# Retention and a Mish layer in one kernel: k cast to fp16 by GpSimd's transfers instead of by ScalarE, from the ninth chunk on

## The chip, the cores and the metric

The kernel runs on one core of a Trainium2 chip. The metric is the device time of one execution in microseconds. Before the change it is 204.29 us, the median of three runs (203.35, 204.29 and 204.36). The engines go by their names in the profile: PE is TensorE's matmul (PEld its weight load), DVE is VectorE, ACT is ScalarE, POOL is GpSimd and SP is SyncE, which here only issues transfers.

## The reference: what is computed

Four batches of eight heads go through a recurrent retention over 768 tokens, with head size 64. The result, as 3072 rows of 512, goes through a two-layer network with the activation h * tanh(softplus(h)) (Mish) between the layers.

```python
gamma = 1.0 - 2.0 ** (-5.0 - np.arange(H))
scale = 1.0 / np.sqrt(D)
for t in range(S):
    state = gamma[None, :, None, None] * state + np.einsum('bhd,bhe->bhde', k[:, :, t], v[:, :, t])
    y[:, :, t] = scale * np.einsum('bhd,bhde->bhe', q[:, :, t], state)
...
h = x @ w_in                                   # 512 x 2048
sp = np.where(h > 20.0, h, np.log1p(np.exp(np.minimum(h, 20.0))))
out = (h * np.tanh(sp)) @ w_out                # 2048 x 512
```

## The kernel before

**Chunks and blocks.** The recurrence is computed in 24 chunks of 128 tokens, six to a batch. Inside a chunk the scores k q^T are masked and multiplied by v ("present"); what came before the chunk enters as the state times q ("past"); the outer products of k and v and a decay give the next state. The decay inside a chunk is put into q and v as a factor per token and head (`qs` and `vs`, tables that the host makes), so k only needs the constant factor `BOOST` = 16, which keeps fp16 in its range. The network divides by BOOST cubed inside the Mish (`inv_boost3`). The network works on blocks of tokens: block 0 has four chunks, and the ten blocks after it have two each (`BLOCKS`, `first`). From block 1 on its first product, and from block 2 on its second too, are done with seven products of half size in place of eight (`g1_seven`, `seven`), which need sums of operands: `x_sums`, `sums_a`, `sums_b`, `sums_c` on VectorE.

**The way of q, k and v.** For chunk g, `load` asks SP for three transfers of 256 KB, each of 128 x 8 rows of 256 bytes. `cast_q` and `cast_v` multiply by the tables and give fp16 on GpSimd; `cast_k` scales by BOOST and gives fp16 on ScalarE (L334). q and k lie side by side in one tile (`qk16`, five buffers), which `turn_by_dma` transposes with one transfer on SP (L351) into `qkt`, where head size lies on partitions. Chunks 0 to 3 have a path of their own (`load_two`, `cast_two`, `turn_two`); chunks 4 and 5 are turned by TensorE.

**The order.** The program's order is written out by hand and each engine works its instructions off in that order. `g1_seven` and `seven` call `step(name)` at named places, and `steps_of(blk)` says which work of the retention stands there, with `a` = the block's first chunk + 4 and `nb` the next block. The places that matter here, in the order of a block:

- *p2*, early in the first product: GpSimd gets `gate_x`, the cast of q of chunk a, the decay of the next block's first state (`decay_next`, L417), the cast of v of chunk a. TensorE gets the outer products of the next block.
- *p6*: SP gets the transpose of chunk a and the loads of chunk a+3 (`turn_and_load`).
- *p7*, *p4*, *end*: stores, the second state's sum, and the sums for the second product on VectorE.
- *h2*: the scores of the next block.
- *m1*, in the second product: ScalarE gets the cast of k of chunk a+1.
- *m2*: GpSimd gets `gate_g`, the decay of the second state, and the casts of q and v of chunk a+1; SP the transpose of chunk a+1.
- *m7*: the next block's y, and ScalarE's cast of k of chunk a+2.
- *m3*: `x_sums` of the next block on VectorE.

A gate (`gate_x`, `gate_g`, L347) is a GpSimd copy of one element of the last result of a group of VectorE's sums. It holds GpSimd's queue until VectorE has done with them.

Block 1 has a half plan of its own: `steps_of_half` in the first product and `plan_of` in the second, which is plain.

Of the kernel before, what the change touches and what calls it, by code (L numbers as in the profile page):

```python
# [16 lines left out]
def kernel(  # L17
# [9 lines left out]
    nc = tc.nc  # L27
# [3 lines left out]
    C = 128  # L31
    NCH = S // C
    NCK = B * NCH
    HP = H // 2
    TB = 512
    CPB = TB // C
# [8 lines left out]
    BOOST = 16.0  # L45
    scale = float(1.0 / np.sqrt(D))
    inv_boost3 = float(1.0 / BOOST**3)

    gamma = (1.0 - 2.0 ** (-5.0 - np.arange(H))).astype(np.float64)
    jj = np.arange(C)  # L50
    mid = (C - 1) / 2.0
    qs_np = np.stack([BOOST * scale * g ** (jj - mid) for g in gamma], 1).astype(np.float32)
    vs_np = np.stack([BOOST * g ** (mid - jj) for g in gamma], 1).astype(np.float32)
    spread = [qs_np[(jj * CPB + r) % C] for r in range(CPB)]
    in_two = [vs_np[(jj % HB) * R + r] for r in range(R)]
# [57 lines left out]
    raw, k16s, v16s, t16s, kts, amf = {}, {}, {}, {}, {}, {}  # L113
    loaded, cast, qkts, ats, ams, states, us, ys, sus = {}, {}, {}, {}, {}, {}, {}, {}, {}
# [3 lines left out]
    nsnap = [0]  # L118
    SEVEN, HALF_SEVEN = 2, 1
    nload, late = [0], []  # L120
    stores = []

    def room(g):
        loaded[g] = [
            lpool.tile([P, H, D], FP32, name=nm + "f", tag=nm + "f", bufs=4 if nm == "q" else 6)
            for nm in "qkv"]

    def load_one(g, n, queue):  # L130
        b, c = divmod(g, NCH)
        queue.dma_start(
            loaded[g][n], (q, k, v)[n][b, :, c * C:(c + 1) * C].rearrange("h p d -> p h d"))

    def load(g):
        room(g)
        for n in (0, 1, 2) if g < CPB + 4 else (1, 0, 2):
            load_one(g, n, nc.sync)

    def load_to(g):  # L140
        while nload[0] < min(g, NCK):
            load(nload[0])
            nload[0] += 1
# [86 lines left out]
    def cast_two(nm, s, half):  # L230
        src = raw.pop((nm, s, half))
        if nm == "k":
            if s not in k16s:
                k16s[s] = castp.tile([P, 2, R, HP, D], FP16, name="qk16")
            nc.scalar.mul(k16s[s][:, half].rearrange("p r h d -> p h r d"), src, BOOST)  # L235
        else:
            v16s[s, half] = castp.tile([P, R, HP, D], FP16, name="v16")
            nc.gpsimd.tensor_tensor(
                v16s[s, half].rearrange("p r h d -> p h r d"), src,
                vs_two[:, half * HP:(half + 1) * HP].unsqueeze(3).broadcast_to((P, HP, R, D)),  # L240
                op=ALU.mult)
# [79 lines left out]
    def room16(g):  # L321
        if g not in cast:
            qk16 = castp.tile([P, 2, H, D], FP16, name="qk16")
            cast[g] = (qk16[:, 0], qk16[:, 1], castp.tile([P, H, D], FP16, name="v16"), qk16)
        return cast[g]

    def cast_q(g):
        if g < NCK:
            nc.gpsimd.tensor_tensor(  # L329
                room16(g)[0], loaded[g][0], qs.unsqueeze(2).broadcast_to((P, H, D)), op=ALU.mult)  # L330

    def cast_k(g):
        if g < NCK:
            nc.scalar.mul(room16(g)[1], loaded[g][1], BOOST)  # L334

    def cast_v(g):
        if g < NCK:
# [3 lines left out]
    def casts(g):  # L341
        cast_q(g)
        cast_k(g)
        cast_v(g)
# [160 lines left out]
    def mish(blk, u, h_ps):  # L505
        nt = BLOCKS[blk] * C
        per = TB // nt
        room = NFB * TB // (2 * nt)
        at0, lies = divmod(u * per, room)
        if lies == 0:  # L510
            gtiles[blk, at0] = gp.tile([P, room, nt], FP16, name="g", tag="g0" if blk == 0 else "g")
        gt = gtiles[blk, at0][:, lies:lies + per]
        nc.scalar.activation(gt, h_ps, AF.Mish, scale=inv_boost3)
        for j in range(per):
            gts[blk, u * per + j] = gt[:, j]
# [288 lines left out]
    def first_block():  # L804
# [15 lines left out]
        first_q_out(0, tq, nc.scalar)  # L820
        tq = [tq, turn_first_q(qf, 1)]
        cast_two("k", 0, 0)
        turn_two(0, 0)
        first_q_out(1, tq[1], nc.vector)
        turned_two(0, 0)
        cast_two("k", 0, 1)
        spin_wide(at, 3)
        scores_half(0, 0, at)
# [3 lines left out]
        for half in range(2):  # L832
            cast_two("v", 0, half)
# [112 lines left out]
    def steps_of(blk):  # L946
        a, nb = first[blk] + 4, blk + 1
        if nb == len(BLOCKS):
            only, then = lambda *work: [], lambda *work: []
        else:  # L950
            only = lambda *work: list(work)
            then = only if a < NCK else lambda *work: []
        return {
            "p2": [*then((gate_x, blk), (cast_q, a)), *only((outer_next, nb), (sum_next, nb, 0),
                   (decay_next, nb, 0)), (cast_v, a)],
            "p6": [(store_due, 1), (turn_and_load, a)],
            "p7": [(store_due, 2), *only((sum_next, nb, 1)), (sums_a, blk, slice(0, FPS))],
            "p4": [(store_due, 3), (sums_a, blk, slice(FPS, FPS + 2))],
            "h2": only((scores, a - 2), (scores, a - 1), (mask, a - 2)),
            "end": [(sums_a, blk, slice(FPS + 2, 2 * FPS))],  # L960
            "m1": [(cast_k, a + 1)],
            "m2": [*only((gate_g, blk), (decay_next, nb, 1)), (cast_q, a + 1), (cast_v, a + 1),
                   *only((mask, a - 1)), (turn_and_load, a + 1)],
            "m7": [*only((y_two, nb)), (cast_k, a + 2)],
            "m3": only((x_sums, nb)),
        }

    def steps_of_half(blk):
        a = first[blk] + 4
        return {  # L970
            "p2": [(gate_x, blk), (cast_v, a - 1)],
            "u2": [(cast_k, a - 1)],
            "p6": [(turn_and_load, a - 1), (some_late, 1)],
            "p7": [(cast_q, a), (some_late, 1)],
            "p4": [(cast_v, a), (some_late, 1), (store, 2)],
            "end": [(cast_k, a), (turn_and_load, a), (store, 2)],
        }

    def plan_of(blk):
        a = first[blk] + 4  # L980
        return {10: [(scores_two, blk + 1)],
                11: [(cast_q, a + 1), (cast_k, a + 1)],
                12: [(outer_two, blk + 1), (cast_v, a + 1), (turn_and_load, a + 1)],
                14: [(y_two, blk + 1)],
                15: [(cast_k, a + 2)]}

    first_block()
    x_sums(HALF_SEVEN)
# [1 line left out]
    for blk in range(1, len(BLOCKS)):  # L990
        if blk >= SEVEN:
            steps = steps_of(blk)
            g1_seven(blk, steps, blk + 1 < len(BLOCKS) and not last_of_batch(first[blk + 1] + 1))
            seven(blk, steps, blk + 1 == len(BLOCKS))
            continue
        g1_seven(blk, steps_of_half(blk))
        n1 = NFB * BLOCKS[blk] // CPB
        plan = plan_of(blk)
        for u in range(n1, 2 * n1):
            store_due(u)  # L1000
            t, part = divmod(u - n1, 4)
            if part == 0:
                o_ps = mmps.tile([P, d_model], FP32, name="o_ps", tag="mm")
            for fb in range(part * 4, part * 4 + 4):
                g2_mm(o_ps, blk, t, fb)
            if part == 3:
                g2_out(o_ps, blk, t, u + 3 if t == 0 else 3)
            for fn, *args in plan.get(u, ()):
                fn(*args)
            some_late(1)  # L1010
        x_sums(blk + 1)
# [31 lines left out]
```

## Time and profile before

| | us |
|---|---|
| median of three runs | 204.29 |
| the profiled execution's own time | 203.41 |
| its span in the profile | 201.2 |
| PE busy | 193.6 |
| DVE busy | 142.3 |
| ACT busy | 111.2 |
| POOL busy | 68.1 |
| a block of two chunks, from 81.4 us on | 14.8 |

Groups of instructions that the change touches, or that stand beside it:

| line, engine | what | count | mean |
|---|---|---|---|
| L334 ACT | cast of k, 128x512 | 20 | 633 ns |
| L235 ACT | cast of k of the first four chunks | 4 | 633 ns |
| L329 POOL | cast of q | 20 | 1207 ns |
| L338 POOL | cast of v | 20 | 1064 ns |
| L417 POOL | decay of a state | 11 | 1270 ns |
| k loads, SP | 256 KB each, from issue to landing | 23 | 4.4 us |
| q loads, SP | 256 KB each | 19 | 4.5 us |
| v loads, SP | 256 KB each | 23 | 5.5 us |
| transpose, SP (L351) | one chunk's q and k | 18 | 4.1 us |

How to read it: spans are of one execution under the profiler, and the time of the same execution lies 2.2 us above its span. The busy time of an engine is the time in which it runs an instruction of work; instructions that only issue a transfer do not count. In a group, "idle before" is the time in which the engine stood still just before its instructions, with what ended it. In the timeline each row gives the start, the duration, the engine, the line, the operation and its tiles, and in brackets the idle time before it. No transfer in this kernel is issued by GpSimd.

### The profile page before, as it was taken

The page shows a single profiled execution, that of the slowest core. Times are in us where ns is not written, and L with a number is a line of the kernel's source. Part 1 is how long each engine was busy: PE and PEld are TensorE (multiplying, and loading weights), DVE is VectorE, ACT ScalarE, POOL GpSimd, SP SyncE. Part 2 cuts the span into 40 slices and gives each one's busy share as a digit, 9 for nine tenths or more (in the row PEclk, how much of TensorE's full clock was granted, in tenths as well). Part 3 has the DMA queues.
Part 4 walks back from the last instruction along what each step waited for, and adds up shares of the span by engine and source line. Part 5 has one row for each costly group of instructions (what it writes and reads, how often), then busy time and mean ns, then how long its engine had stood idle before and what let it go on. Part 6 is the DMA issues. An engine that isn't in the chain of part 4 may idle for free.

```text
span 201.2 us, 5425 instructions
## 1 busy us (share of the span) xinstructions
PE 193.6 (96%) x2239; PEld 152.5 (76%) x2239; DVE 142.3 (71%) x271; ACT 111.2 (55%) x199; POOL 68.1 (34%) x83
## 2 busy tenths in 40 slices
PE   6897999999999999999999999999999999999993
PEld 2355544455965888988988988988988988988982
DVE  2787793958839696787696695787696695595552
ACT  2363665243970874674674674674664763753840
POOL 4072000529324417514407607603406616200000
PEclk9999999999999999999999999999999999999999
DMA  5999999999999999997992993999993923200202
GB/s 169 302 312 359 385 387 302 271 263 205 210 180 269 279 221 195 199 227 166 215 194 72 232 230 73 232 190 153 241 200 57 235 81 55 104 3 30 79 26 78
DMA packets 95896, 38.65 MB, mean 192 GB/s; under 512 B 82304, under 2 KB 89984, under 8 KB 95872
## 3 DMA queue, kind: packets, MB, share of 16 engines
q1 hardware_dynamic: 92608, 37.50, 84.3%
q10 hardware_dynamic: 3264, 0.82, 2.3%
q8 instruction: 17, 0.28, 0.6%
q14 instruction: 7, 0.06, 0.1%
HBM read 27.30 MB, written 6.29 MB: 167 GB/s over the span
## 4 chain that ended last, share of the span: by engine, by line
PE 91%; ACT 2%; DMA 2%; DVE 2%; issue 1%; DVEq 0%
PE o_ps L727 28%; PE h_ps L656 18%; PE h_ps L632 16%; PE o_ps L519 10%; PE h_ps L497 6%; PE y_ps L436 3%; PE at L386 3%; DMA qfirst<-in_q_dram 2%; PE y_ps L426 2%; PE u_ps L400 2%; ACT xt L482 1%; PE h_ps L800 1%; DVE qfirst L204 1%; DVE am L274 1%; ACT qk L235 1%
## 5 line engine op out<-in xcount | busy, mean ns | idle before, releaser
L656 PE MATMUL h_ps<-xt,win 128*128 128x256 f16 x320 | 41.2, 273 | 0.0
L329 POOL TENSOR_TENSOR qk<-qf,qvs 128x512 f16<-128x512 f32 x20 | 24.1, 1207 | 25.3 <-DMA qf<-in_q_dram 23.4
L656 PEld LDWEIGHTS <-win 128*128 128x128 f16 x320 | 29.3, 98 | 3.7
L727 PEld LDWEIGHTS <-gsum 128*128 128x128 f16 x288 | 27.5, 98 | 4.0
L649 DVE TENSOR_TENSOR hsum<-h_ps,hsnap 128x512 f32<-128x512 f32 x30 | 19.8, 688 | 13.7 <-PE h_ps L632 11.5
L392 DVE TENSOR_TENSOR am<-at,tri 128x1024 f16<-128x1024 f32 x20 | 24.2, 1217 | 3.9 <-PE at L386 3.9
L660 ACT ACTIVATE g<-h_ps 128x512 f16<-128x512 f32 x40 | 23.7, 593 | 5.6 <-PE h_ps L656 5.5
L727 PE MATMUL o_ps<-tmat,gsum 128*128 128x256 f16 x216 | 25.1, 273 | 0.0
L639 ACT COPY hsnap<-h_ps 128x512 f32<-128x512 f32 x30 | 16.6, 588 | 13.9 <-PE h_ps L632 13.9
L338 POOL TENSOR_TENSOR v<-vf,qvs 128x512 f16<-128x512 f32 x20 | 21.3, 1064 | 5.3 <-PE u_ps L400 3.9
L727 PEld LDWEIGHTS <-g 128*128 128x128 f16 x216 | 21.1, 98 | 2.5
L741 DVE TENSOR_TENSOR osb<-o_ps,snap 128x256 f32<-128x256 f32 x27 | 11.4, 424 | 16.1 <-PE o_ps L727 11.3
L519 PE MATMUL o_ps<-wout,g 128*128 128x512 f16 x96 | 22.7, 380 | 0.0
L643 ACT ACTIVATE g<-hsum 128x512 f16<-128x512 f32 x30 | 18.7, 634 | 4.0 <-DVE hsum L649 4.0
L482 ACT CAST xt<-y_ps 128x1024 f16<-128x1024 f32 x10 | 10.1, 1012 | 19.1 <-PE y_ps L436 19.1
L632 PEld LDWEIGHTS <-wsum 128*128 128x128 f16 x320 | 19.1, 98 | 0.5
L733 ACT COPY snap<-o_ps 128x256 f32<-128x256 f32 x27 | 10.0, 372 | 15.7 <-PE o_ps L727 15.7
L334 ACT ACTIVATE qk<-kf 128x512 f16<-128x512 f32 x20 | 12.7, 633 | 8.4 <-DMA kf<-in_k_dram 8.4
L727 PE MATMUL o_ps<-wout,g 128*128 128x256 f16 x144 | 17.2, 273 | 0.0
L632 PE MATMUL h_ps<-xsum,wsum 128*128 128x128 f16 x240 | 16.7, 219 | 0.0
L347 POOL COPY gate<-gsum 128x1 f16<-128x1 f16 x8 | 1.5, 186 | 44.2 <-DVE gsum L701 44.2
L632 PEld LDWEIGHTS <-win 128*128 128x128 f16 x240 | 15.1, 98 | 1.5 <-issue 0.8
(96 smaller groups left out, 288.3 us busy)
## 6 DMA issues: line engine op xcount, KB each, us to landing
kf<-in_k_dram SPq DMA_DIRECT2D x23, 256.0 KB, 4.4
vf<-in_v_dram SPq DMA_DIRECT2D x23, 256.0 KB, 5.5
out_dram<-osb SPq DMA_DIRECT2D x22, 256.0 KB, 4.3
qf<-in_q_dram SPq DMA_DIRECT2D x19, 256.0 KB, 4.5
wt<-in_moe_w_out_dram SPq DMA_DIRECT2D x3, 1024.0 KB, 8.7
wi<-in_moe_w_in_dram SPq DMA_DIRECT2D x4, 512.0 KB, 7.2
wi<-in_moe_w_in_dram SPq DMA_DIRECT2D x2, 1024.0 KB, 11.1
qfirst<-in_q_dram SPq DMA_DIRECT2D x2, 512.0 KB, 5.2
```

The source lines that it names most:

```text
L329: nc.gpsimd.tensor_tensor(room16(g)[0], loaded[g][0], qs.unsqueeze(2).broadcast_to((P, H, D)), op=ALU.mult)
L334: nc.scalar.mul(room16(g)[1], loaded[g][1], BOOST)
L338: nc.gpsimd.tensor_tensor(room16(g)[2], loaded[g][2], vs.unsqueeze(2).broadcast_to((P, H, D)), op=ALU.mult)
L392: nc.vector.tensor_tensor(am, ats.pop(g), tri.unsqueeze(1).unsqueeze(1).broadcast_to((P, 2, HP, C)), op=ALU.mult)
L519: nc.tensor.matmul(o_ps, gts[blk, fb][:, t * P:(t + 1) * P], wouts[s][:, f, cols], start=(fb == 0), stop=(fb == NFB - 1))
L632: nc.tensor.matmul(h_ps[:, f], w(f, d), x(d), start=first and f == 0 and d == 0, stop=d == n - 1, skip_group_check=True)
L639: nc.scalar.copy(x, h_ps)
L643: nc.scalar.activation(gt[:, 2 * i * FPS:(2 * i + 1) * FPS, j * P:(j + 1) * P], h, AF.Mish, scale=inv_boost3)
L649: nc.vector.tensor_tensor(h, h_ps, x, op=ALU.add)
L656: nc.tensor.matmul(h_ps[:, j], win(s, 2 * half + j, bp), xt(blk, bp), start=bp == 0, stop=bp == NBP - 1)
L660: nc.scalar.activation(gt[:, fb:fb + 2], h_ps, AF.Mish, scale=inv_boost3)
L727: nc.tensor.matmul(o_ps, x(f), w(f), start=first and f == 0, stop=f == n - 1, skip_group_check=True)
```

## The change

For chunks 8 to 23 (`BRING` = 8) the load of k into an fp32 tile and its scaling by ScalarE are left out. In their place `bring_k` has GpSimd issue one transfer that reads k's fp32 rows from HBM and writes fp16 straight into k's half of the `qk16` tile. The factor BOOST that k had goes into the table of q, for all chunks; the casts of k that remain (chunks 0 to 7) are plain copies. SP's loads for these chunks are q and v alone. `bring_k` stands last in GpSimd's sequence at p2 (for chunk a+1) and at m2 (for chunk a+2), half a block ahead of the casts of the same chunk's q; in block 1 it stands at p2, at p4 and in step 12 of `plan_of`.

```diff
-    qs_np = np.stack([BOOST * scale * g ** (jj - mid) for g in gamma], 1).astype(np.float32)
+    qs_np = np.stack([BOOST**2 * scale * g ** (jj - mid) for g in gamma], 1).astype(np.float32)
...
+    BRING = CPB + 4
...
     def room(g):
         loaded[g] = [
             lpool.tile([P, H, D], FP32, name=nm + "f", tag=nm + "f", bufs=4 if nm == "q" else 6)
-            for nm in "qkv"]
+            if g < BRING or nm != "k" else None for nm in "qkv"]
...
-        for n in (0, 1, 2) if g < CPB + 4 else (1, 0, 2):
+        for n in (0, 1, 2) if g < BRING else (0, 2):
             load_one(g, n, nc.sync)
...
-            nc.scalar.mul(k16s[s][:, half].rearrange("p r h d -> p h r d"), src, BOOST)
+            nc.scalar.copy(k16s[s][:, half].rearrange("p r h d -> p h r d"), src)
...
+    def bring_k(g):
+        if g < NCK:
+            b, c = divmod(g, NCH)
+            nc.gpsimd.dma_start(
+                room16(g)[1], k[b, :, c * C:(c + 1) * C].rearrange("h p d -> p h d"))
+
     def cast_k(g):
-        if g < NCK:
-            nc.scalar.mul(room16(g)[1], loaded[g][1], BOOST)
+        if g < BRING:
+            nc.scalar.copy(room16(g)[1], loaded[g][1])
...
             "p2": [*then((gate_x, blk), (cast_q, a)), *only((outer_next, nb), (sum_next, nb, 0),
-                   (decay_next, nb, 0)), (cast_v, a)],
+                   (decay_next, nb, 0)), (cast_v, a), (bring_k, a + 1)],
...
-            "m1": [(cast_k, a + 1)],
             "m2": [*only((gate_g, blk), (decay_next, nb, 1)), (cast_q, a + 1), (cast_v, a + 1),
-                   *only((mask, a - 1)), (turn_and_load, a + 1)],
-            "m7": [*only((y_two, nb)), (cast_k, a + 2)],
+                   (bring_k, a + 2), *only((mask, a - 1)), (turn_and_load, a + 1)],
+            "m7": only((y_two, nb)),
...
-            "p2": [(gate_x, blk), (cast_v, a - 1)],
+            "p2": [(gate_x, blk), (cast_v, a - 1), (bring_k, a)],
             "u2": [(cast_k, a - 1)],
...
-            "p4": [(cast_v, a), (some_late, 1), (store, 2)],
-            "end": [(cast_k, a), (turn_and_load, a), (store, 2)],
+            "p4": [(cast_v, a), (bring_k, a + 1), (some_late, 1), (store, 2)],
+            "end": [(turn_and_load, a), (store, 2)],
...
-                11: [(cast_q, a + 1), (cast_k, a + 1)],
-                12: [(outer_two, blk + 1), (cast_v, a + 1), (turn_and_load, a + 1)],
-                14: [(y_two, blk + 1)],
-                15: [(cast_k, a + 2)]}
+                11: [(cast_q, a + 1)],
+                12: [(outer_two, blk + 1), (cast_v, a + 1), (bring_k, a + 2),
+                     (turn_and_load, a + 1)],
+                14: [(y_two, blk + 1)]}
```

## The prediction

> **What bounds the kernel now.** I read the page first: the busy shares, and the shares of the chain that ended last.
>
> ```profile
> PE 193.6 (96%) x2239; PEld 152.5 (76%) x2239; DVE 142.3 (71%) x271; ACT 111.2 (55%) x199; POOL 68.1 (34%) x83
> ...
> PE 91%; ACT 2%; DMA 2%; DVE 2%; issue 1%; DVEq 0%
> ```
>
> TensorE is on 91% of the chain; ScalarE, whose work is taken away, on 2%. An average says little of a place, so next the busy time by stretches, cut where blocks of two chunks begin.
>
> ```profile
> core 0: us, PE busy (x) PEld busy (x) DVE busy (x) ACT busy (x) POOL busy (x), PEclk, DMA share, GB/s
> ...
> 81.40:96.20 14.80, 14.80 (x192) 13.23 (x190) 11.10 (x23) 9.14 (x17) 5.63 (x7) 1.00 0.95 201
> 96.20:111.00 14.80, 14.80 (x193) 13.30 (x191) 11.10 (x24) 9.14 (x17) 6.06 (x7) 1.00 0.92 156
> 111.00:125.90 14.90, 14.90 (x195) 13.40 (x193) 10.97 (x24) 9.14 (x17) 7.32 (x8) 1.00 0.90 178
> ```
>
> A block takes 14.80 us and TensorE is busy in all of it, at a granted clock of 1.00; ScalarE is busy 9.14. GpSimd's 5.63 to 7.32 leave it about 8 us, and the list of waits says for what it stands still:
>
> ```profile
> POOL gate L347 <- DVE gsum L701: 44.2, 8, 6.9
> ...
> POOL gate L347 <- DVE xsum L608: 21.6, 8, 5.2
> ```
>
> These are the two gates per block. Last, the timeline around one of each:
>
> ```profile
> 79.06 1.04 POOL L338 TENSOR_TENSOR v<-vf,qvs 128x512 f16<-128x512 f32 x1
> ...
> 80.53 0.63 ACT L334 ACTIVATE qk<-kf 128x512 f16<-128x512 f32 x1
> ...
> 80.94 0.28 DVE L605 TENSOR_TENSOR xsum<-xt 128x256 f16<-128x256 f16 x1
> ...
> 81.57 0.58 SPq L132 DMA_DIRECT2D qf<-in_q_dram  x1
> ...
> 82.09 0.19 POOL L347 COPY gate<-xsum 128x1 f16<-128x1 f16 x1 [1.99 <-DVE xsum L608]
> ...
> 82.39 1.06 PE L632 MATMUL h_ps<-xsum,wsum 128*128 128x128 f16 x16
> ...
> 83.90 1.27 POOL L417 TENSOR_TENSOR st<-su,gcm 128x512 f16<-128x512 f32 x1 [0.64 <-DVE su L412]
> ...
> 85.13 1.04 POOL L338 TENSOR_TENSOR v<-vf,qvs 128x512 f16<-128x512 f32 x1
> ...
> 91.02 0.19 POOL L347 COPY gate<-gsum 128x1 f16<-128x1 f16 x1 [4.84 <-DVE gsum L701]
> ```
>
> Both new places are in it. After m2's cast of v (ends 80.10) GpSimd is free until the gate at 82.09: 1.99 us. After p2's (ends 86.17) it is free until 91.02: 4.84 us. Other blocks leave 1.76 to 3.69 and 4.83 to 6.91.
>
> **The change part by part.** *Taken from ScalarE:* sixteen scalings of k (chunks 8 to 23) at 633 ns, 10.1 us in all. Worth nothing: ScalarE waits for TensorE on both sides of them (its next copy, at 81.92, had waited 0.75 us for the matmuls), and TensorE waits for none. If that cover were gone, one would cost 0.63.
>
> *Taken from SP's queue:* sixteen loads of 256 KB, each holding the queue for at least 0.57 us. Nothing: q and v are asked for 1.5 blocks, some 20 us, before their casts and land in 4.5 and 5.5 us. Only chunk 8 shows a late q (GpSimd waits 2.66 us at 60.77), and TensorE is busy through it.
>
> *Turned from scaling into copying:* eight casts of the first chunks, two on the chain at the start (L235, 1%). Copies of 128x512 stand at 585 to 588 ns against 633: -0.05 each, -0.1 together. The factor in q is in a table and costs nothing.
>
> *Added to GpSimd:* sixteen casting transfers, three in block 1, two in each of blocks 2 to 7, one in block 8. GpSimd issues no transfer in this trace, so the time D that one holds it is bounded by other rows. Below: SP issues the same 1,024 rows of 256 bytes in 0.57 us. Between: a cast of 512 elements per partition takes 1.04 us, 2.0 ns an element step; one such step for each of 1,024 rows is 2.1 us. Above: four steps a row, 8.3 us. I take 2.1, as that row is GpSimd's own.
>
> What it may cost: at m2 the gate at 82.09 would open at 82.2, 0.1 late. Behind the gate stand the cast of q, the decay of the state, the cast of v. The cast of q may slip by 0.64 us, as the decay waits that long for VectorE's sum. The decay ends at 85.17; VectorE reads it in the sum at p7, which it reaches at 86.2, after the second of two `hsum` additions that start at 84.93 (1.29 us). So D is free up to about 1.99 + 0.64 + 1.0 = 3.6 us there. At p2 the gate leaves 4.84, and the decay behind it is read by VectorE only in the next block, 5 us later: free to 8 and more. On average two transfers and 6.14 us of other work (the mean of five blocks) fit into 14.82 us while D is under 4.3. Cost at 2.1: 0.
>
> *The transfer's own waits.* Its buffer was last read five chunks earlier, by that chunk's transpose and outer products, over a block back; so it waits for nothing. The transpose on SP now waits for its landing. Asked for at 80.1, with 2.1 to issue and a landing as of the loads (4.4), k is there at 86.6, where the transpose now issues at 84.28: 2.3 us late. Behind it on SP stand two loads with some 15 us in hand and stores with five buffers. The transpose takes 4.1 us to land and is read by the scores one block later, at about 102.3: hidden, with over 10 us left. The one at m2 (92.22) finds its k landed, as that was asked for at 86.2.
>
> *Bytes.* Reads of HBM stay; what is written to the k tiles is halved. The transfer engines' share of 0.95 per block says nothing of a bound, since 201 GB/s move here and 381 in the stretch from 20 to 33 us.
>
> **The sum:** -0.1 + 0 = -0.1 us on the profiled execution's 203.41 (span 201.2, 2.2 around it). That run lies 0.88 below the median of the three, 204.29, and at their lower end, so a median of new runs is 204.2. Unknown beside it: what a program pays for a transfer queue that it had not used, at its start or end. Bounds: nothing, and 1 us (about half of the 2.2 outside the span). Own range 203.1 to 205.3.
>
> **Rivals.** *1. GpSimd becomes the bound (slower).* Place: both transfers of blocks 2 to 7. It decides from D = 3.6 in tight blocks and 4.3 in all. At 5.5: 2 x 5.5 + 6.14 - 14.82 = 2.3 us a block, by six blocks 14, less about 4 of slack at the start: +10, so 214. At 8.3 it is 7.9 a block, some 250. For it: each transfer has 1,024 rows, and the only issuer with a row, SP, is another engine. Against it: GpSimd's own 2.0 ns an element step, by which D stays under 3.6. The Trainium skill (DMA: Bandwidth & Descriptors, "Anatomy of one DMA") calls the generation small, with many descriptors before its cost shows; by that D is nearer 1 us than 5, an estimate from that page, and this rival falls. No row here shows it, and the chance below is set without it.
>
> *2. Issuing holds VectorE's additions (slower).* The trace shows that the two engines hinder each other: GpSimd's cast of q takes 1.51 us beside VectorE's `gsum` (L705) and 1.04 alone, and L705 itself 0.68 or 1.43. If issuing a transfer does the same, the four additions of `x_sums` (80.94 to 81.96) wait at m2 until 82.2, TensorE's product at 82.39 finds its operand (the second of them) at 82.8, and the next `hsum` is 1.1 late: 0.4 to 1.1 a block, say 0.8. Only four of the six m2 places run into them (casts of v end at 80.10, 109.85, 124.59, 154.34); at the others, 93.19 and 137.68, `x_sums` comes over 2.5 us later. 4 x 0.8 = +3.2: 207.5; it decides from D = 1.7 on (0.84 until the additions start, plus 0.84 that the second, which ends at 81.55, may slip). The Trainium skill (SBUF — State Buffer, "Who interferes with whom") gives the rule against it: VectorE's additions of two SBUF tensors hinder only GpSimd work that reads SBUF, and descriptors are written, not read (it calls this inferred). By that rule the price is 0; the trace agrees as far as casts, which read, are hindered.
>
> *3. Faster.* ScalarE, SP and the transfers get freer, and a wait hidden inside TensorE's busy time goes. In the last block, with nothing beside it, the 56 products of L727 take 6.13 us; the 56 of L632 at 0.89 for 16 are 3.12, the 32 of L656 at 0.87 for 8 are 3.48; the scores 0.56, present 0.57, past and outer products 0.45 each: 14.76 against 14.80. So 0.04 by nine blocks and the 0.3 us of idle time from 33 to 81 us are all there is: 203.6.
>
> **Chances.** No change as summed: 0.48 (same 0.39, slower 0.07, faster 0.02). Rival 1: 0.29. Rival 2: 0.16. Rival 3: 0.07 (faster 0.03, same 0.04). Half a per cent, 1.0 us, is the spread of the three runs (203.35 to 204.36) and what counts as no change. So faster 0.05, same 0.43, slower 0.52: the single likeliest case is no change, though the slower ones together weigh more. The range starts at 203.1 and goes up to 216, through rival 2 and rival 1 with D up to 5.8; beyond lie some 0.15.
>
> **What would show it.** Right: blocks of 14.8 us with TensorE busy in all of them, GpSimd's gates still waiting for VectorE, no cast of k on ScalarE. Rival 1: the gates wait for nothing, GpSimd's queue is solid, VectorE waits for `st`. Rival 2: `xsum` additions long or late beside the m2 transfers, TensorE idle before L632 on `wsum`. The forecast falls if a transfer held GpSimd over 3.6 us, or if k landed over 10 us after it was asked for.

## The result, and the profile after

The changed kernel takes 203.36 us, the median of 20 runs (202.86 to 204.04); the kernel before takes 203.94 beside it (20 runs, 203.23 to 204.88). The ratio is 0.9972, with a 95% interval of 0.996 to 0.9985. That is 0.28% faster: inside the half per cent that the prediction called no change, but with an interval that leaves 1 out. The profiled execution of the changed kernel took 204.0 us with a span of 202.2, so it is one of its longer ones, and its total cannot be set against before's 203.41 and 201.2. Two of the eight runs of experiment 5, 207.2 and 207.4 us long at a granted clock of 0.992, fell in the slower state that executions of a program can have, and its numbers leave them out.

The page of the changed kernel gives the busy shares and the chain:

```profile
PE 193.7 (96%) x2239; PEld 153.0 (76%) x2239; DVE 143.9 (71%) x271; ACT 102.6 (51%) x183; POOL 82.4 (41%) x99
...
PE 80%; DMA 8%; DVE 6%; ACT 2%; issue 1%; SPq 0%; DVEq 0%
```

Sixteen instructions have left ScalarE (111.2 to 102.6 us) and sixteen have come to GpSimd (68.1 to 82.4; the time in which GpSimd issues a transfer is counted in its busy time, unlike SP's). TensorE's work is the same. It holds a smaller share of the chain, 80% for 91%, because in this execution it stood still once, early on, and the chain before that runs through the landing of weights and VectorE's sums. That is not the change's doing: the unchanged kernel of experiment 1 shows the same 80%. The busy time by stretches shows where:

```profile
core 0: us, PE busy (x) PEld busy (x) DVE busy (x) ACT busy (x) POOL busy (x), PEclk, DMA share, GB/s
33.00:49.00 16.00, 15.04 (x97) 7.17 (x95) 12.39 (x13) 4.58 (x7) 6.83 (x6) 1.00 1.15 241
81.40:96.20 14.80, 14.80 (x190) 13.26 (x189) 11.11 (x22) 8.10 (x16) 8.06 (x10) 1.00 1.17 182
96.20:111.00 14.80, 14.80 (x191) 13.30 (x190) 11.03 (x23) 8.16 (x16) 7.06 (x9) 1.00 0.88 141
111.00:125.90 14.90, 14.90 (x194) 13.42 (x192) 11.03 (x23) 8.03 (x16) 9.26 (x11) 1.00 1.07 161
```

The blocks still begin 14.80 us apart and TensorE is busy in all of them, with 1 us less on ScalarE and 1 to 2.4 us more on GpSimd. The 0.96 us without TensorE lie from 33 to 49 us, before the first new transfer (53.80 us). Experiment 7 deals with them.

GpSimd's two gates, in the list of waits (total, times, longest, in us):

```profile
POOL gate L354 <- DVE gsum L708: 37.9, 8, 6.0
...
POOL gate L354 <- DVE xsum L615: 14.7, 8, 3.2
```

They were 44.2 and 21.6. So 13.2 of the 15.2 us that GpSimd now spends on sixteen transfers (15 at 0.94, the first 1.08) came out of its waiting. The timeline of GpSimd, at the place that the prediction used:

```profile
80.09 1.04 POOL L345 TENSOR_TENSOR v<-vf,qvs 128x512 f16<-128x512 f32 x1
81.07 0.94 POOL L336 DMA_DIRECT2D qk<-in_k_dram  x1
83.12 0.18 POOL L354 COPY gate<-xsum 128x1 f16<-128x1 f16 x1 [1.11 <-DVE xsum L615]
...
84.99 1.27 POOL L424 TENSOR_TENSOR st<-su,gcm 128x512 f16<-128x512 f32 x1 [0.43 <-DVE su L419]
...
87.20 0.94 POOL L336 DMA_DIRECT2D qk<-in_k_dram  x1
92.05 0.18 POOL L354 COPY gate<-gsum 128x1 f16<-128x1 f16 x1 [3.91 <-DVE gsum L708]
```

Where 1.99 and 4.84 us were idle, 1.11 and 3.91 still are, with a transfer of 0.94 in each place.

The queues of the transfers (packets, MB, share of 16 engines) and two rows of the issues (size of each, median us to landing):

```profile
q1 hardware_dynamic: 75968, 33.30, 73.1%
q0 software_dynamic: 16640, 2.10, 16.4%
...
qk<-in_k_dram POOLq DMA_DIRECT2D x16, 128.0 KB, 5.4
...
qkt<-qk SPq DMA_TRANSPOSE x18, 4.5
```

Before, q1 alone had 92,608 packets and 84.3%. By these two profiles the sixteen plain loads of k took 0.843 x 201.2 - 0.731 x 202.2 = 21.8 us of the sixteen engines' time, and the casting ones take 0.164 x 202.2 = 33.2 us: the same 16,640 packets at 31.9 ns each for 21.0, though only half the bytes are written. The first figure is a difference of two large ones and is rough. Over six profiles with the plain loads alone q1 took 83.0% to 88.6%, and over four with the changed kernel's loads 72.9% to 74.2%; that leaves the plain loads 18 to 31 us, while the casting transfers took 33 to 37. So casting took more in every pairing, by a factor that is not settled. The transposes land in 4.5 us for 4.1, which is no more than the spread between profiles: 3.9 to 4.4 in the six, 4.1 to 4.5 in the four.

### The profile page after: what moved, and what is told of

Same layout as the page of the kernel before. It is cut to its first block, busy times and chain, and to the rows that moved or that the text cites. A ratio compares the mean times of both kernels' runs of the same rounds, so it can differ in the third digit from the quotient of the medians.

```text
span 202.2 us, 5401 instructions
## 1 busy us (share of the span) xinstructions
PE 193.7 (96%) x2239; PEld 153.0 (76%) x2239; DVE 143.9 (71%) x271; ACT 102.6 (51%) x183; POOL 82.4 (41%) x99
## 3 DMA queue, kind: packets, MB, share of 16 engines
q0 software_dynamic: 16640, 2.10, 16.4%
## 4 chain that ended last, share of the span: by engine, by line
PE 80%; DMA 8%; DVE 6%; ACT 2%; issue 1%; SPq 0%; DVEq 0%
PE o_ps L734 28%; PE h_ps L663 18%; PE h_ps L639 16%; DMA wt<-in_moe_w_out_dram 6%; PE o_ps L526 6%; PE y_ps L443 3%; PE at L393 3%; DMA qfirst<-in_q_dram 2%; PE y_ps L433 2%; PE u_ps L407 2%; DVE tmat L558 1%; PE h_ps L807 1%; ACT xt L489 1%; DVE tmat L560 1%; DVE tmat L559 1%
## 5 line engine op out<-in xcount | busy, mean ns | idle before, releaser
L424 POOL TENSOR_TENSOR st<-su,gcm 128x512 f16<-128x512 f32 x11 | 13.9, 1267 | 6.1 <-DVE su L419 6.1
```

The source lines that it names most:

```text
L424: by.tensor_tensor(states[g], sus.pop(g), gcm, op=ALU.mult)
```

## The experiments

Each run stands beside runs of the kernel before on the same chip; "outside the span" is a run's time less its span, as the median of a kernel's runs. Where a transfer, a fill or a load is added, nobody reads what it writes.

### 1. The kernel before, unchanged

> The kernel before, unchanged, timed as if it were another kernel: ratio 1.000, its interval shows what a difference of 0.3% is worth. Time minus span: 2.2 us as in the profiled run of before (203.41 - 201.2) if that is a property of the kernel and the change takes 0.4 us off it (after: 204.0 - 202.2 = 1.8); 1.8 us if that was one execution's.

203.84 us (12 runs) against 203.79 (35 runs); 1.0007 [0.9993, 1.0022]. A pair of equal kernels differs by 0.1%, so the 0.28% is not noise. This run's profile is of use too: span 202.0 and 0.64 us without TensorE from 33 to 49 us, where the profile used for the prediction had 0.04. That profile was one of before's quick executions.

### 2. The copies alone, and the transfers alone

To before, the factor in q and copies for scalings, all loads and casts of k kept:

```diff
-            nc.scalar.mul(k16s[s][:, half].rearrange("p r h d -> p h r d"), src, BOOST)
+            nc.scalar.copy(k16s[s][:, half].rearrange("p r h d -> p h r d"), src)
...
-            nc.scalar.mul(room16(g)[1], loaded[g][1], BOOST)
+            nc.scalar.copy(room16(g)[1], loaded[g][1])
```

> Before, with the factor of k moved to q's table and ScalarE's casts of k as plain copies, all loads and casts kept. Theory A (the gain of the change is at the start, where two casts of k lie on the chain): most of 0.28%, 0.4 to 0.6 us. Theory B (the gain comes from the transfers, which take loads off SP's queue and the transfer engines while the weights are still arriving): -0.1 us as summed in the prediction, 0.05%. Theory C (it is noise): ratio 1.000.

203.76; 1.0001 [0.9986, 1.0016]; outside the span 1.99. The other half, from the changed kernel, with its eight copies turned into scalings by 1:

```diff
-            nc.scalar.copy(room16(g)[1], loaded[g][1])
+            nc.scalar.mul(room16(g)[1], loaded[g][1], 1.0)
```

(and the same in the cast of the first chunks; what the transfers replace stays left out).

> After, with ScalarE's casts of the first eight chunks as scalings by 1.0, the instruction that before used, in place of copies. Theory A: the gain is gone, ratio within 0.1% of 1. Theory B: it keeps 0.2% or more. With one copy gone from the sum, -0.1 us less than after.

203.36; 0.9977 [0.9957, 0.9997]; outside the span 1.79. The gain comes with the transfers and what they replace; the copies alone show none.

### 3. Every transfer twice

```diff
+            for _ in range(1):
+                spare = lpool.tile([P, H, D], FP16, name="kf", tag="kf", bufs=6)
+                nc.gpsimd.dma_start(
+                    spare, k[b, :, c * C:(c + 1) * C].rearrange("h p d -> p h d"))
```

> After, with every casting transfer issued a second time into an unused tile. A transfer holds GpSimd for 0.94 us in after's trace, so two hold 1.9: under the 3.6 that the prediction found free at m2, so blocks stay at 14.8 us and the time within 0.2% of after. The second one runs into x_sums at m2 (it ends some 1.9 us after the cast of v, the additions start 0.84 after it): if issuing holds VectorE's additions (rival 2), L612 to L615 get longer than 0.28 and blocks grow by 0.3 to 0.8 us, 2 to 5 us in all; if not, they stay at 0.28.

204.06; 1.0014 [0.9997, 1.003], so 0.7 us are lost again. The test of rival 2 is in the timeline of GpSimd and VectorE at m2 (first GpSimd's transfers, then VectorE's additions of `x_sums`; two answers of the trace):

```profile
81.48 0.94 POOL L336 DMA_DIRECT2D qk<-in_k_dram  x1
82.42 0.88 POOL L340 DMA_DIRECT2D kf<-in_k_dram  x1
```

```profile
82.38 0.28 DVE L616 TENSOR_TENSOR xsum<-xt 128x256 f16<-128x256 f16 x1
82.70 0.29 DVE L617 TENSOR_TENSOR xsum<-xt,xsum 128x256 f16<-128x256 f16 x1
82.91 0.28 DVE L618 TENSOR_TENSOR xsum<-xt 128x256 f16<-128x256 f16 x1
83.11 0.28 DVE L619 TENSOR_TENSOR xsum<-xt,xsum 128x256 f16<-128x256 f16 x1
```

The additions lie under the second transfer and take the 0.28 us that they took without one; in all ten blocks they take 0.28 to 0.29. Issuing does not hold them. What was lost, TensorE's weight loads show:

```profile
73.50 0.23 PEld L397 LDWEIGHTS <-qkt 64*128 64x128 f16 x8 [0.21 <-issue]
74.26 0.23 PEld L397 LDWEIGHTS <-qkt 64*128 64x128 f16 x8 [0.53 <-DMA qkt<-qk]
```

In the block from 66.16 to 81.06 the scores of chunk 9 wait for its transpose, which took 7.5 us to land. This block takes 14.90 us for 14.37 in the kernel before, which is 0.53 of the 0.7; the later blocks are as long as before (14.73 to 14.97).

### 4. GpSimd held longer by each transfer

Four fills of an unread tile behind each transfer (0.94 + 2.29 = 3.23 us), and then eight (0.94 + 4.62 = 5.56 us):

```diff
+            spare = lpool.tile([P, H, D], FP32, name="kf", tag="kf", bufs=6)
+            for _ in range(4):
+                nc.gpsimd.memset(spare, 0.0)
```

> After, with GpSimd held longer at every new place by four fills of an unused tile behind the transfer (about 0.5 us each, 2.1 in all), and no added traffic: D is about 3.0 to 3.3. The prediction found 3.6 free at the tight m2 places, so: blocks 14.8 us, the time within 0.2% of after (203.2 to 203.8). If the slack is smaller than worked out, VectorE waits for st (L424 by the old count) and blocks grow.

203.45 (10 runs) against 203.72 (25 runs); 0.9989 [0.998, 0.9998]. GpSimd's timeline with four:

```profile
80.50 0.94 POOL L336 DMA_DIRECT2D qk<-in_k_dram  x1
81.44 2.29 POOL L340 MEMSET kf<- 128x512 f32 x4
83.68 0.19 POOL L357 COPY gate<-xsum 128x1 f16<-128x1 f16 x1
```

The gate behind m2's transfer no longer waits for anything, and the kernel is no slower than before: 3.23 us are free.

> The same with eight fills: D about 5.0 to 5.7, over the 3.6 at m2 and the mean of 4.3. Rival 1's own price: 2 x 5.4 + 6.14 - 14.82 = 2.1 us a block at six blocks, less about 4: +5 to +10 us, 208 to 214, GpSimd's gates waiting for nothing. If the time stays at after's, the slack was far larger than the prediction had it and rival 1's price was wrong.

222.32 (220.96 to 223.7, 4 runs); 1.0913 [1.0867, 1.0958]. GpSimd's timeline with eight, and then the waits from 60 to 200 us:

```profile
78.15 4.62 POOL L340 MEMSET kf<- 128x512 f32 x8
82.71 0.19 POOL L357 COPY gate<-gsum 128x1 f16<-128x1 f16 x1
```

```profile
DVE su L422 <- POOL st L427: 9.9, 3, 3.8
...
PE at L396 <- DVE su L422: 7.4, 3, 3.0
```

Now the gate behind p2's transfer does not wait either, VectorE waits for the decayed state and TensorE for VectorE: rival 1 to the letter, 18.6 us dear. GpSimd's work of a block is then 2 x 5.56 + 6.14 = 17.26 us, and the seven blocks from 65.65 to 186.91 us take 17.32 on average. Behind its first standstill of 3.0 us TensorE was granted a clock of 0.50 to 0.51 from 76 to 82 us; that hardly sets the time, as a run with a mean clock of 0.992 took 220.96 us and the profiled one, at 0.976, 221.28. The threshold lies between 3.23 and 5.56 us, and the real transfer, at 0.94, far under it.

### 5. SP's loads kept

The changed kernel, with SP still loading k of chunks 8 to 23 into tiles that nobody reads:

```diff
-            if g < BRING or nm != "k" else None for nm in "qkv"]
+            for nm in "qkv"]
...
-        for n in (0, 1, 2) if g < BRING else (0, 2):
+        for n in (0, 1, 2) if g < BRING else (1, 0, 2):
```

> After, with SP's sixteen loads of k kept, into tiles that nobody reads. If the time outside the span shrank because SP has fewer transfers, it is 2.04 again; if because GpSimd has some, 1.78. Inside the span: if the freed transfer engines are worth something, blocks or the stretch from 49 to 82 us lose it again (as with e4_twice, 0.5 us, scores waiting for a transpose); if not, the time of after, 203.4.

204.58 (6 runs, 204.1 to 205.59) against 203.72; 1.005 [1.0029, 1.007]. The changed kernel with four fills, on the same chip, took 203.45, 1.1 us less. The queue of SP, and then TensorE's weight loads:

```profile
67.76 2.56 SPq L358 DMA_TRANSPOSE qkt<-qk  x1
```

```profile
75.30 0.23 PEld L393 LDWEIGHTS <-qkt 64*128 64x128 f16 x8 [2.05 <-DMA qkt<-qk]
```

The transpose of chunk 9 is issued at 67.76 and lands 7.5 us later, at 75.26; TensorE has waited 2.05 us, and this block takes 16.42 us for 14.37. Leaving out SP's loads is thus not worth nothing: it pays for the new transfers. How near the edge this transpose stands in the changed kernel itself, its own SP queue and weight loads show:

```profile
66.42 1.49 SPq L358 DMA_TRANSPOSE qkt<-qk  x1
```

```profile
73.62 0.45 PEld L393 LDWEIGHTS <-qkt 64*128 64x128 f16 x16 [0.21 <-issue]
```

It lands after 6.6 us, at 73.0; the second eight weight loads, which need it, start at 73.85. In hand: 0.8 us. In the profile of before that the prediction used, it was issued at 65.3, landed at 69.8 and was needed at 72.8: 3.0 us. That difference is not shown to be the change's. In experiment 1's profile of the same kernel before, the transpose is issued at 66.23, lands after 6.0 us and has 1.3 us in hand. Four variants of the kernel before (experiments 2, 6 and 7) have 0.8 to 0.9, and three of the changed kernel with its own transfers alone (experiments 2, 4 and 7) 2.7 to 3.3. From one execution to the next it moves by some 2 us, with the change or without.

### 6. What lies outside the span

The changed kernel's runs have 1.78 us outside the span (1.73 to 1.85), those of before 2.04, 2.07 and 2.15 in three sets of 35, 25 and 15 (13 of these 75 single runs stand at 1.74 to 1.81). To see which part does it, the kernel before was given one small casting transfer of 128 rows on GpSimd ahead of block 1, and then sixteen, one behind each cast of k:

```diff
+    one = cpool.tile([P, D], FP16, name="one")
...
             nc.scalar.mul(room16(g)[1], loaded[g][1], BOOST)
+            if g >= CPB + 4:
+                nc.gpsimd.dma_start(one, k[0, 0, :P])
```

> Before, with one added casting transfer of 128 rows by GpSimd, into an unused tile, as block 1 begins. The kernels without a transfer of GpSimd have 2.04 us between time and span, those with it 1.78. If it is the use of that queue, this one has 1.78 too and the time is 0.26 us under before (0.13%); if it is the number of instructions or of SP's transfers, 2.04 and the time of before.

203.72 against 203.72; 0.9997 [0.9989, 1.0006]; outside the span 2.03.

> Before, with sixteen added casting transfers of 128 rows by GpSimd, one behind each cast of k of chunks 8 to 23, into an unused tile; loads and ScalarE's casts are kept. One such transfer left 2.03 us between time and span, sixteen large ones with ScalarE's casts gone 1.78, with or without SP's loads. If sixteen transfers make it, 1.78 here; if the missing work of ScalarE does, 2.04. Inside the span 0 to 0.3 us more than before.

203.49 (11 runs) against 203.76 (15); 0.9988 [0.9979, 0.9997]; outside the span 1.80 (1.73 to 1.82). With all of ScalarE's and SP's work on k in place, sixteen transfers from GpSimd bring 0.27 us, and one brings nothing. There are two levels: with sixteen transfers or more every run on record stands at the lower one (at most 1.85), and without them only a run now and then. What in the sixteen does it, their number or that they go on until late in the program, stays open.

### 7. The early stall

The changed kernel's 0.96 us from 33 to 49 us, in VectorE's timeline:

```profile
40.42 1.53 DVE L558 TENSOR_TENSOR tmat<-wout 128x1024 f16<-128x1024 f16 x1
41.87 0.68 DVE L384 COPY qkt<-t_ps 128x1024 f16<-128x1024 f16 x1
```

A sum of weights (`some_late`) stands ahead of the copy of chunk 4's turned q and k, and takes 1.53 us beside one of GpSimd's casts of q (0.68 in the profile that the prediction used). TensorE's scores wait for the copy, 0.92 us. One of these sums was moved to block 1, in the changed kernel and in the kernel before:

```diff
-            if NFB <= u < NFB + 5:
+            if NFB <= u < NFB + 4:
                 some_late(1)
```

> After, with one of VectorE's sums of the output weights (the first of the second half, L558, 1.53 us beside a cast of q) moved from block 0 into block 1, so that the copy of the turned chunk 4 does not wait for it. In the profiles of after, e1, e2, e3 TensorE idles 0.6 to 1.0 us from 33 to 49 us, in after 0.9 of it until that copy. If that idle time is what spreads the runs (spans of after 201.1 to 202.3), the stretch loses under 0.2 us and the median falls by 0.4 to 0.7 us, to 202.7 to 203.0, with a smaller spread. If the weights' landing sets it, nothing changes: 203.4.

202.71 (202.3 to 202.74, 5 runs) against 203.76; 0.9946 [0.9932, 0.996]. Stretch and VectorE's timeline:

```profile
33.00:49.00 16.00, 15.96 (x120) 8.06 (x118) 11.75 (x13) 4.54 (x6) 7.62 (x7) 1.00 1.17 242
```

```profile
40.55 0.69 DVE L384 COPY qkt<-t_ps 128x1024 f16<-128x1024 f16 x1 [0.77 <-PE t_ps L382]
```

> The same move in the kernel before. If the two gains are independent, the median falls by 0.4 to 0.7 us from 203.8 as well, and e10 stays some 0.3 to 0.5 us under it. If the gain of the change was all in that stretch, the two come out alike.

202.95 (202.56 to 203.17, 5 runs); 0.996 [0.9947, 0.9972]. The copy now waits for its input and not for the sum, and the stall is gone: 0.04 us are left in both profiles. As the prediction's profile had 0.04 without the move, it is the medians that show what the move is worth. Without the stall the two kernels have equal spans, 200.90 us as the median of each, and differ by what lies outside: 1.81 against 2.07. The changed kernel with this one number altered has the lowest median of all, below both kernels of the case; the ranges of the two sets of five runs overlap.

## Why the prediction was right or wrong

**The case.** The likeliest case, no change, came out: 203.36 for 204.2. Of the 0.84 us between them, about 0.35 is the starting point. The prediction took the median of three runs, 204.29, and 20 and 35 runs of before give 203.94 and 203.79. The rest, 0.49, is a gain that the sum, at -0.1, did not have.

**TensorE covers ScalarE's work.** Right. Sixteen casts, 8.6 us of busy time by the page, went from ScalarE, and steady blocks kept their 14.8 us. One trace of a gain inside the span is left: between the seventh and the eighth copy of a block's output to `xt` lie 14.81 to 14.83 us in the profiles of six kernels with ScalarE's casts of k (before and five variants, the sixteen small transfers of experiment 6 among them) and 14.73 to 14.74 in six without. That is 0.08 us, once; how it comes about was not found.

**The time that a transfer holds GpSimd.** The mis-sized term: 2.1 us were taken, 0.94 measured, between the lower bound of 0.57 and the value taken. The row chosen, a cast's 2.0 ns an element step, did not carry over; SP's row was nearer. The miss cost nothing, as both values lie under the slack. The Trainium skill (DMA: Bandwidth & Descriptors, "Anatomy of one DMA") calls the generation small, and the trace agrees: 0.94 us for 1,024 rows and 0.59 for 128 in experiment 6, so 0.35 us for eight times the rows.

**The slack of 3.6 us at m2 and rival 1.** The mechanism was right, and experiment 4 brackets the threshold between 3.23 us (free) and 5.56 us (+18.6). The price of the rival was too low: +10 was forecast at 5.5. Its price for a block was right: 2 x 5.56 + 6.14 - 14.82 = 2.4 us, and 17.32 - 14.82 = 2.5 were measured. What failed is the count, six blocks where the excess comes in seven, and the 4 us of slack taken off at the start: already the first of the seven took 20.95 us for 14.37, and no gate of GpSimd waited any more after the one at 52.04.

**Rival 2.** Refuted by experiment 3. The Trainium skill (SBUF — State Buffer, "Who interferes with whom") gives the rule that VectorE's additions of two SBUF tensors hinder only GpSimd work that reads SBUF; the trace agrees, with 0.28 to 0.29 us under a transfer.

**The transpose, "hidden, with over 10 us left".** True in the steady blocks. There the transpose issues 6.5 us behind the start of the cast of v (80.09 to 86.58), for 5.2 before and 7.5 forecast. The microsecond between is the shorter hold: k is there 5.4 us after its transfer is issued, 0.94 of it the hold, where the forecast had 2.1 + 4.4. The step did not look at chunk 9, brought in block 1 for scores that are computed in block 2. It has no 10 us: 0.8 in this profile, and 0.8 to 3.3 in others with the change and without. The change alone did not use that up; experiments 3 and 5, with more transfers, did.

**SP's loads, "nothing".** Wrong as a reason, right as a sum: without their removal the change costs 0.5% (experiment 5). The prediction said that the share of the transfer engines bounds nothing. It bounds no steady block, but one transpose that lands after 7.5 us is a wait of 2.05. The load taken off and the load put on cancelled, and as the prediction weighed neither, that was luck.

**The copies.** Forecast -0.05 us each, measured -0.01: the casts of k take 622 ns for 633. The row used, 585 to 588, was of copies that read PSUM. Either is nothing (experiment 2).

**The new queue, 0 to +1 us.** Wrong sign: -0.26 us outside the span (experiment 6). With the 0.08 us above it is the only part of the gain that is shown; of the 0.58 us between 203.94 and 203.36 some 0.24 stay without a cause, and before's own median moves from 203.72 to 203.94 between sets. The spans' medians, 201.6 for the changed kernel and 201.6 to 201.9 for before in three sets, cannot be told apart.

**Rival 3, "0.3 us of idle time are all there is".** Read from one quick execution. Experiment 1's execution of the same kernel idles for 0.64 us in the stretch from 33 to 49 us alone, and the variants of it in experiments 2 and 6 for 0.79 to 1.08; there was more to win than the profile showed, but not by this change (experiment 7).

## What to carry to other kernels

Work taken from an engine that waits on the busiest engine was worth nothing here; judge a transfer moved to another queue by the slack in front of what it makes late, and look for that slack where the pipeline starts, not in a steady block. A transfer that casts spares an engine's instruction but took more of the transfer engines' time than the plain load (33 to 37 us for sixteen, against 18 to 31), and beside the loads instead of in their place it cost 0.5%. Before trusting the idle time or the slack in one profile, profile the same kernel a second time: here the stall worth more than the change showed up only then, and the slack of one transpose was 3.0 us in one profile of the kernel before and 1.3 in the other.

## What was not expected of the hardware

Sixteen transfers issued by GpSimd, of 1,024 rows or of 128, shorten what lies outside the span from between 1.99 and 2.15 us to between 1.77 and 1.81, and one transfer does not (2.03). Where the casting transfers are doubled, or come beside SP's loads, the transposes' median landing is 6.0 and 5.3 us, and the longest takes 7.5. In the changed kernel and its variants without added traffic the median is 4.1 to 4.5 and the longest 7.0, with the plain loads alone 3.9 to 4.4 and 6.0. Whether the longer packets make them late, or the queue's order, was not tried.
